# Windowed attention with sinks, then a maxout feed-forward layer: the prologue in a new order, and the stores one slot later

## The chip, the core and the metric

The kernel runs on one core of a Trainium2 chip. A core has five engines that run their own instruction streams and meet through semaphores: TensorE (PE, matrix products; its weight loads are shown as PEld), VectorE (DVE), ScalarE (ACT), GpSimd (POOL) and SyncE (SP, which here only issues transfers). Transfers (DMAs) are issued by SP, POOL and, at the end, ACT. Results of TensorE land in PSUM, of which this kernel uses eight buffers in turn; everything else lives in SBUF.

The metric is device time in microseconds (us). Before the change it is 181.4 us, the median of 4 runs from 181.05 to 181.6. A profile belongs to one of these runs.

## The reference

The attention part has 4 sequences (batch), 8 heads, 768 positions and head size 64. Each position sees the 128 positions up to and with itself, and the first 4 positions of the sequence (the sinks):

```python
scores = scale * np.matmul(q, k.transpose(0, 1, 3, 2))
is_sink = pos[None, :] < n_sink
in_window = (rel >= 0) & (rel < window)
a = softmax(np.where(is_sink | in_window, scores, -1e9))
attn = np.matmul(a, v)
x = attn.transpose(0, 2, 1, 3).reshape(3072, 512)
h = np.maximum(np.maximum(x @ w1, x @ w2), x @ w3)     # 512 -> 768
out = h @ w_out                                        # 768 -> 512
```

Inputs and the output are float32; the kernel computes with bfloat16 operands.

## The kernel before, in words

The 3072 rows are cut into 12 chunks of 256 positions, three chunks to a sequence. A chunk goes through the same steps, each a short letter in the kernel's own script (`step`, L453): K and Q (transpose k and q to `kk` and `qT`), B (open the PSUM banks of the scores with an additive mask, by matmuls against `ident`), S (scores of a pair of heads and their exponentials, tiles `st` and `e_sb`), M (mask the exponentials by a product on VectorE), Z and V (scores and values of the sinks), A (one pair of heads: probabilities times values into `o_ps`, then reciprocal and scaling on VectorE into `x_sb`), T (transpose `x_sb` to `xT`), F0 to F8 (one third of one of the three feed-forward products each, 8 matmuls into `h_ps`; weight 0 is taken by ScalarE's copy, weights 1 and 2 by VectorE's maximum), Y or W (output product `y_ps`, ScalarE's copy to `y_sb`, and the store), D (transposes of k and q by DMA), E (placing the transposed k), L (loads), X (sink keys). `Fa6` is step F6 of chunk `a`.

There is no scheduler. The whole program stands in an order written out by hand: strings of such steps (L497 to L563), mixed with casts and loads that are called by name. Every engine runs its instructions in the order in which they are issued there, and a wait at the head of an engine's stream holds up all behind it. The eight PSUM buffers are handed out in turn, so a step can also wait for the reader of an older tile.

The program has a prologue and slots. The prologue (L501 to L548) brings chunks 0, 1, 2 and 3 in. Chunk 0 comes by plain loads on SP; k and q of chunks 1 and 2 come as `runs` by transfers on POOL's queue that also cast to bfloat16 (L84), and so do the weights (L162, L170). POOL's stream is: build `ident` and the masks `msk` and `msk0` (L135 to L146), issue runs of chunk 1, v of chunk 1 and weight 0, build `sel` and `v_sink` (L178), cast the sink values `vs_raw` (L520), copy the sink keys, issue weights 1 and 2, cast v of chunk 1, issue chunk 2 and the output weight. `warm` matmuls (L124) fill PE's waits. Chunk 0's AV (`Aa0` to `Aa3`) stands before K and Q of chunk 1.

A slot i (L550 to L563) holds the feed-forward of chunk i, the AV of chunk i+1, the scores of chunk i+2, the DMA transposes of chunk i+3 and the loads of chunk i+4. Step T is 4 transposes on PE and a ScalarE copy for each half up to chunk 4 (L374), and a DMA transpose issued by SP (L375) from chunk 5 on. The store of a chunk is issued on SP at the end of its output step (L425). Slot 3 has a step order of its own (L557), with one F step more ahead of the AV and T at its end.

Of the kernel before, what the change touches and what calls it, by code (L numbers as in the profile page):

```python
# [16 lines left out]
def kernel(  # L17
# [13 lines left out]
    nc = tc.nc  # L31
    B, H, S, D = q.shape
# [3 lines left out]
    d_ff = moe_w1.shape[1]  # L36
# [14 lines left out]
    with tc.manual_schedule():  # L51
# [84 lines left out]
        for i in range(2):  # L136
            for slot, op, sign in ((1, ALU.is_ge, 1), (0, ALU.is_gt, -1)):
# [1 line left out]
                nc.gpsimd.affine_select(  # L139
                    out=m, in_=m, compare_op=op, fill=0.0, base=-sign * i,  # L140
                    pattern=[[sign, 2], [2 * sign, 64]], channel_multiplier=-2 * sign)
        nc.gpsimd.tensor_copy(msk[:, 2:4], msk[:, 0:2])
        msk0 = const.tile([128, 3, 128], BF16, name="msk0")
        nc.gpsimd.tensor_copy(msk0, msk[:, 1:4])
        for i in range(2):
            nc.gpsimd.memset(msk0[64 * i:64 * i + n_sink // 2, 0:2], 1.0)  # L146


        msb = const.tile([128, 4, 128], BF16, name="msb")
# [130 lines left out]

        sts = {}

        def score_banks(ci, pairs):

            for p in pairs:
                sts[ci, p] = [psum.tile([128, 4, 128], F32, tag="f", name="st") for _ in range(2)]
                for st in sts[ci, p] if ci < 2 else ():
                    nc.tensor.matmul(st if ci else st[:, 1:], lhsT=ident, rhs=msb if ci else msb0,  # L288
                                     start=True, stop=False, skip_group_check=True)

        def score(ci, pairs):

            b, c = divmod(ci, CPB)
            kc, kp = kk[ci % (2 * CPB)], kk[(ci - 1) % (2 * CPB)]
            half = [slice(64 * h, 64 * h + 64) for h in range(2)]
            if (ci, pairs[0]) not in sts:
                score_banks(ci, pairs)
            for p in pairs:
                st = sts[ci, p]
                qh = qT[ci % (2 * CPB)][:, :, p].rearrange("p i (n t) -> p n i t", n=2)  # L300
                parts = [(slice(1, 3), kc, 0, qh), (slice(3, 4), kc, 128, qh[:, 1])]
                if c > 0:
                    parts.insert(0, (slice(0, 1), kp, 128, qh[:, 0]))
                for sl, kx, k0, qx in parts:
                    for h, r in enumerate(half):
                        nc.tensor.matmul(st[h][:, sl], lhsT=kx[r, p, k0:k0 + 128], rhs=qx[r],  # L306
                                         start=ci >= 2, stop=True, skip_group_check=ci < 2)
            lo = 0 if c > 0 else 1
            for p in pairs:
                e = es[ci, p] = work.tile([128, 2, 4, 128], BF16, tag="e", bufs=8, name="e_sb")  # L310
                for h, st in enumerate(sts.pop((ci, p))):
                    nc.scalar.activation(e[:, h, lo:], st[:, lo:], AF.Exp, scale=scale)  # L312
# [58 lines left out]
        def xpose(ci, t):  # L371
            if t == 0:
                xTs[ci] = work.tile([128, 2, DS, 128], BF16, tag="xT", bufs=3, name="xT")
            if ci > CPB + 1:  # L374
                nc.sync.dma_start_transpose(  # L375
                    out=xTs[ci][:, t], in_=xs[ci][:, t].rearrange("p h d -> p (h d)"))
                return
            pt = psum.tile([128, DS, 128], BF16, tag="f", name="xt_ps")
            x = xs[ci][:, t].rearrange("p h d -> p (h d)")
            for ds in range(DS):  # L380
                nc.tensor.transpose(pt[:, ds], x[:, ds * 128:(ds + 1) * 128], ident)  # L381
            copy = nc.vector.tensor_copy if ci == 0 else nc.scalar.copy
            copy(xTs[ci][:, t], pt)  # L383
# [26 lines left out]
        def ffn_y(ci, ts, fbs):  # L410

            for t in ts:
                yps[ci, t] = psum.tile([128, d_model], F32, tag="f", name="y_ps")
            for part in fbs:
                for t in ts:
                    for fb in part:
                        nc.tensor.matmul(yps[ci, t], lhsT=hs[ci][:, fb, t * 128:(t + 1) * 128],  # L417
                                         rhs=wo[:, fb], start=(fb == 0), stop=(fb == FB - 1))
            for t in ts:
                if t == 0:  # L420
                    ys[ci] = work.tile([128, 2, d_model], F32, tag="y", bufs=3, name="y_sb")
                y = ys[ci]
                nc.scalar.copy(y[:, t], yps.pop((ci, t)))  # L423
                if t == 1:
                    store(y, ci, slice(0, 2))  # L425

        def ffn_y_end(ci):

# [24 lines left out]
        def step(op):  # L453
# [12 lines left out]
            elif name == "S":  # L466
                score(ci, [int(x) for x in arg])
            elif name == "B":
                score_banks(ci, [int(x) for x in arg])
            elif name == "M":  # L470
                mask(ci, [int(x) for x in arg])
            elif name == "Z":
# [11 lines left out]
                xpose(ci, int(arg))  # L484
            elif name == "F":
                ffn_h(ci, int(arg))
            elif name == "Y":
                ffn_y(ci, [int(arg)], [range(FB)])
            elif name == "W" and ci == NCH - 1:
# [4 lines left out]
        def run(text, **at):  # L494
# [3 lines left out]

        load_runs(1)  # L501
        load_v(1, nc.gpsimd)
        load_w(0, 0, 256)
        load_w(0, 256, d_ff)
        sink_v_init()
        warm(36)
        cast_qk(0, 0, 0, nc.vector)
        cast_qk(0, 1, 0, nc.vector)
# [2 lines left out]
        warm(4)  # L511
        run("Qa0 Ba01", a=0)
        cast_qk(0, 0, 1, nc.vector)
        mask_terms(msk, msb)
        cast_qk(0, 1, 1, nc.vector)
        run("Ka1 Sa01 Qa1 Ba23", a=0)
        run("Sa23", a=0)
        cast_v(0, 0, nc.vector)
        cast_v(0, 1, nc.vector)
        nc.gpsimd.tensor_copy(v_sink[:, :, 0:D], vs_raw)  # L520
        sink_k(0, nc.gpsimd.tensor_copy)
        load_w(1, 0, 256)
# [22 lines left out]
        run("Fb5 Sc23 Mc23 Fb8 Vc Ac0 Ac1 Ya0 Ya1", a=0, b=1, c=2)  # L545
        cast(4)
        run("Ac2 Ac3 Yb0 Tc0 Tc1 Kd0 Qd0 Kd1 Qd1 Yb1", b=1, c=2, d=3)
        run("Zd Sd0123 Md0123 De Lf", d=3, e=4, f=5)  # L548

        for i in range(2, NCH):  # L550
            if i + 3 < NCH:
                cast(i + 3)
            text = "Fa0 Fa1 {} Fa2 {} Zc Sc0123 Mc0123 Wa0"
            if i == 2:
                text = text.format("", "Vb Ab0 Fa3 Ab1 Xb Fa4 Ab2 Fa5 Ab3 Fa6 Dd Le Fa7 Fa8 Ya0 Ec Tb0 Tb1 Ya1")
                text = text.replace(" Wa0", "")
            elif i == CPB:  # L557
                text = text.format("Ec", "Fa3 Vb Ab0 Fa4 Ab1 Fa5 Ab2 Fa6 Ab3 Dd Le Fa7 Fa8 Tb0 Tb1")
            elif i < 0:
                text = text.format("Ec", "Vb Ab0 Fa3 Xb Ab1 Fa4 Ab2 Fa5 Ab3 Fa6 Dd Le Fa7 Tb0 Tb1 Fa8")  # L560
# [41 lines left out]
```

## Time and profile before

| Quantity | Value |
|---|---|
| Median of 4 runs | 181.4 us |
| The profiled execution | 181.6 us, with a span of 179.9 us from first to last instruction |
| PE busy | 171.3 us (95% of the span), granted clock 0.996 |
| DVE / ACT / POOL busy | 116.0 / 90.1 / 69.5 us |
| Feed-forward products, L396 | 864 matmuls, busy 103.5 us |
| Output products, L417 | 132 matmuls, busy 30.7 us |
| HBM traffic | 25.20 MB read, 6.29 MB written |

A busy share is an average over the whole run; what a change in one place is worth is read from that place. A line of the chain of waits holds a start, a duration and the work that was last to end there. A line of the timeline holds start, duration, engine, line of the code, instruction, operands and count, and in brackets how long the engine stood idle before it and for whom. Matmuls are pipelined, so the duration of a group (8 matmuls of 256 columns in 0.87 us in the chain) says more than the mean of one.

### The profile page before, as it was taken

How to read it: one execution, taken by the hardware profiler on the slowest of the kernel's cores; microseconds unless marked ns; L12 is line 12 of the kernel's file. 1: busy time of each engine (PE TensorE's matmuls, PEld its weight loads, DVE VectorE, ACT ScalarE, POOL GpSimd, SP SyncE). 2: the span in 40 equal slices, each digit the busy share in tenths (PEclk: the TensorE clock that was granted, in tenths of full speed). 3: DMA queues.
4: the chain of work that ended last, by engine and by line, in shares of the span. 5: the costliest groups of instructions: out<-in, count | busy, mean ns of one | idle time of the engine just before them, and what ended most of it. 6: DMA issues, size and time to landing. Idle time of an engine off the chain costs nothing.

```text
span 179.9 us, 4911 instructions
## 1 busy us (share of the span) xinstructions
PE 171.3 (95%) x1998; PEld 131.8 (73%) x1998; DVE 116.0 (64%) x245; ACT 90.1 (50%) x191; POOL 69.5 (39%) x121
## 2 busy tenths in 40 slices
PE   6869999999999999999999999999999999999991
PEld 6545888775697688588598688686796796796880
DVE  1786435687289189677667776786595785673551
ACT  2346852572971872951933924914736726622220
POOL 7909910657902394655023525336136200000001
PEclk9999999999999999999999999999999999999998
DMA  5999999999599998993799998999999935122404
GB/s 150 225 213 197 205 209 211 225 295 287 145 196 254 200 256 265 194 290 119 141 255 264 157 278 230 107 294 259 132 287 249 124 93 62 41 79 58 117 0 117
DMA packets 64645, 33.63 MB, mean 187 GB/s; under 512 B 26640, under 2 KB 60944, under 8 KB 64624
## 3 DMA queue, kind: packets, MB, share of 16 engines
q1 hardware_dynamic: 59520, 27.70, 66.5%
q0 software_dynamic: 4864, 5.38, 17.4%
q8 instruction: 15, 0.25, 0.6%
q10 hardware_dynamic: 240, 0.26, 0.6%
q14 instruction: 6, 0.05, 0.1%
HBM read 25.20 MB, written 6.29 MB: 175 GB/s over the span
## 4 chain that ended last, share of the span: by engine, by line
PE 84%; DMA 5%; ACT 4%; DVE 2%; POOL 2%; issue 2%; POOLq 0%; ACTq 0%
PE h_ps L396 50%; PE y_ps L417 16%; PE o_ps L358 6%; DMA runs<-in_k_dram 5%; PE st L306 3%; ACT e_sb L312 3%; DVE h_sb L402 2%; PE y_ps L436 2%; PE pt L251 1%; PE xt_ps L381 1%; PE st L288 1%; PE o_ps L345 1%; PE sk L325 1%; POOL msk L139 1%; ACT xT L383 1%
## 5 line engine op out<-in xcount | busy, mean ns | idle before, releaser
L396 PE MATMUL h_ps<-xT,w 128*128 128x256 bf16 x864 | 103.5, 273 | 0.3
L396 PEld LDWEIGHTS <-w 128*128 128x128 bf16 x864 | 81.3, 98 | 11.9 <-issue 1.4
L402 DVE TENSOR_TENSOR h_sb<-h_sb,h_ps 128x512 bf16<-128x512 bf16 x72 | 49.1, 684 | 27.1 <-PE h_ps L396 21.0
L312 ACT ACTIVATE e_sb<-st 128x512 bf16<-128x512 f32 (+1 forms) x96 | 45.2, 595 | 7.3 <-PE st L306 7.3
L400 ACT CAST h_sb<-h_ps 128x512 bf16<-128x512 f32 x36 | 22.0, 615 | 45.3 <-PE h_ps L396 45.3
L319 DVE TENSOR_TENSOR e_sb<-e_sb,msk 128x1024 bf16<-128x1024 bf16 (+1 forms) x40 | 28.7, 720 | 19.0 <-ACT e_sb L312 18.6
L203 POOL CAST qk_bf<-qk_raw 128x512 bf16<-128x512 f32 x36 | 22.7, 637 | 44.9 <-DMA qk_raw<-in_k_dram 31.9
L212 POOL CAST ve<-v_raw 64x512 bf16<-64x512 f32 x44 | 30.8, 700 | 20.9 <-DMA v_raw<-in_v_dram 18.0
L417 PE MATMUL y_ps<-wo,h_sb 128*128 128x512 bf16 x132 | 30.7, 379 | 0.3
L417 PEld LDWEIGHTS <-h_sb 128*128 128x128 bf16 x132 | 12.4, 97 | 14.0 <-issue 1.1
L366 DVE TENSOR_TENSOR x_sb<-o_ps,rc 128x256 bf16<-128x256 f32 x48 | 20.4, 425 | 1.7
L358 PE MATMUL o_ps<-ve,e_sb 128*128 128x65 bf16 x352 | 17.6, 194 | 0.6 <-DVE ve L212 0.6
L358 PEld LDWEIGHTS <-e_sb 128*128 128x128 bf16 x352 | 15.5, 97 | 2.6 <-issue 0.7
L423 ACT COPY y_sb<-y_ps 128x512 f32<-128x512 f32 x22 | 12.6, 636 | 9.6 <-PE y_ps L417 9.5
L407 POOL DMA_DIRECT2D out_dram<-y_sb x1 | 0.6, 571 | 35.1 <-ACT y_sb L447 35.1
L306 PE MATMUL st<-qT,kk 64*128 64x128 bf16 (+1 forms) x256 | 13.6, 237 | 0.2
L306 PEld LDWEIGHTS <-kk 64*128 64x128 bf16 x256 | 8.8, 94 | 4.8 <-issue 3.0
L363 DVE RECIPROCAL rc<-o_ps 128x4 f32<-128x4 f32 x48 | 8.5, 176 | 3.8 <-PE o_ps L358 3.6
L128 PE MATMUL warm<-ident 128*128 128x128 bf16 x56 | 5.2, 265 | 1.4 <-POOL ident masks.py:199 1.4
L256 ACT CAST qT<-pt 128x512 bf16<-128x512 f32 x4 | 2.1, 588 | 8.0 <-PE pt L251 8.0
L330 ACT ACTIVATE e_sink<-sk 128x256 bf16<-128x256 f32 x8 | 3.2, 395 | 5.6 <-PE sk L325 5.6
L128 PEld LDWEIGHTS <-ident 128*128 128x128 bf16 x56 | 4.6, 122 | 1.6 <-POOL ident masks.py:199 1.4
(58 smaller groups left out, 74.0 us busy)
## 6 DMA issues: line engine op xcount, KB each, us to landing
out_dram<-y_sb SPq DMA_DIRECT2D x22, 256.0 KB, 4.1
qk_raw<-in_k_dram SPq DMA_DIRECT2D x20, 256.0 KB, 4.2
qk_raw<-in_q_dram SPq DMA_DIRECT2D x20, 256.0 KB, 4.7
v_raw<-in_v_dram SPq DMA_DIRECT2D x10, 512.0 KB, 6.3
v_raw<-in_v_dram POOLq DMA_DIRECT2D x2, 512.0 KB, 10.3
w<-in_moe_w_dram POOLq DMA_DIRECT2D x2, 512.0 KB, 9.7
w<-in_moe_w_dram POOLq DMA_DIRECT2D x1, 768.0 KB, 11.7
wo<-in_moe_w_out_dram POOLq DMA_DIRECT2D x2, 384.0 KB, 12.9
```

What stands on the lines that cost most here:

```text
L203: (eng.tensor_copy if eng else nc.scalar.copy)(dst.rearrange("p i (h d) -> p h i d", d=D), src)
L212: (eng.tensor_copy if eng else nc.scalar.copy)(dst[64 * i:64 * i + 64], src[64 * n:64 * n + 64, :, i])
L306: nc.tensor.matmul(st[h][:, sl], lhsT=kx[r, p, k0:k0 + 128], rhs=qx[r], start=ci >= 2, stop=True, skip_group_check=ci < 2)
L312: nc.scalar.activation(e[:, h, lo:], st[:, lo:], AF.Exp, scale=scale)
L319: nc.vector.tensor_tensor(out=e, in0=e, in1=m, op=ALU.mult)
L358: nc.tensor.matmul(o[:, t, h], lhsT=es[ci, p][:, h, sl], rhs=ve[b % 2][:, n, 2 * p + h], start=(c == 0 and x == 0), stop=(x == len(blocks) ...
L366: nc.vector.tensor_mul(xs[ci][:, :, 2 * p:2 * p + 2], o[:, :, :, 0:D], rc.unsqueeze(3).to_broadcast([128, 2, 2, D]))
L396: nc.tensor.matmul(hp[:, f], lhsT=w_sb[wi, 2 * fp + f][:, ds], rhs=xTs[ci][:, :, ds], start=(ds == 0), stop=(ds == DS - 1))
L400: nc.scalar.copy(dst, hp)
L402: nc.vector.tensor_max(dst, dst, hp)
L417: nc.tensor.matmul(yps[ci, t], lhsT=hs[ci][:, fb, t * 128:(t + 1) * 128], rhs=wo[:, fb], start=(fb == 0), stop=(fb == FB - 1))
L423: nc.scalar.copy(y[:, t], yps.pop((ci, t)))
```

## The change

Ten edits, all of them in the order of work or in who does it:

- the copies that finish `msk` and `msk0` move from POOL to DVE, and `sink_v_init` moves to the head of POOL's issues;
- in chunk 0's preparation, the last q cast goes ahead of the second mask term;
- half of chunk 0's v casts move from DVE to POOL;
- the first two thirds of weight 1 are issued before the cast of the sink values, the last third after the v casts of chunk 1;
- 6 `warm` matmuls in place of two times 8; K of chunk 1 goes ahead of chunk 0's AV, Q of chunk 1 stands in its middle, T of chunk 0 comes after the first scores of chunk 1;
- pairs 0 and 1 of chunk 1 are masked by DVE products (M) in place of the additive matmuls (B);
- Tb comes one F step later, and `Fa7` directly after it;
- T of chunk 4 is done by DMA transposes;
- slot 3 takes the same step order as the later slots;
- stores are a step of their own (O) that lags: chunk 0's comes at the end of the prologue, and in slot i the store of chunk i-1 after the loads.

```diff
-        nc.gpsimd.tensor_copy(msk[:, 2:4], msk[:, 0:2])
+        nc.vector.tensor_copy(msk[:, 2:4], msk[:, 0:2])
...
-        nc.gpsimd.tensor_copy(msk0, msk[:, 1:4])
+        nc.vector.tensor_copy(msk0, msk[:, 1:4])
         for i in range(2):
-            nc.gpsimd.memset(msk0[64 * i:64 * i + n_sink // 2, 0:2], 1.0)
+            nc.vector.memset(msk0[64 * i:64 * i + n_sink // 2, 0:2], 1.0)
...
-        def score_banks(ci, pairs):
+        def score_banks(ci, pairs, mb=None):
...
-                for st in sts[ci, p] if ci < 2 else ():
-                    nc.tensor.matmul(st if ci else st[:, 1:], lhsT=ident, rhs=msb if ci else msb0,
+                for st in sts[ci, p] if mb is not None else ():
+                    nc.tensor.matmul(st if ci else st[:, 1:], lhsT=ident, rhs=mb,
...
-                                         start=ci >= 2, stop=True, skip_group_check=ci < 2)
+                                         start=not opened, stop=True, skip_group_check=opened)
...
-            if ci > CPB + 1:
+            if ci > CPB:
                 nc.sync.dma_start_transpose(
...
                 nc.scalar.copy(y[:, t], yps.pop((ci, t)))
-                if t == 1:
-                    store(y, ci, slice(0, 2))
...
+            elif name == "O":
+                store(ys[ci], ci, slice(0, 2))
...
+        sink_v_init()
         load_runs(1)
         load_v(1, nc.gpsimd)
         load_w(0, 0, 256)
         load_w(0, 256, d_ff)
-        sink_v_init()
...
+        cast_qk(0, 1, 1, nc.vector)
         mask_terms(msk, msb)
-        cast_qk(0, 1, 1, nc.vector)
         run("Ka1 Sa01 Qa1 Ba23", a=0)
         run("Sa23", a=0)
         cast_v(0, 0, nc.vector)
-        cast_v(0, 1, nc.vector)
-        nc.gpsimd.tensor_copy(v_sink[:, :, 0:D], vs_raw)
+        cast_v(0, 1, nc.gpsimd)
         sink_k(0, nc.gpsimd.tensor_copy)
         load_w(1, 0, 256)
-        load_w(1, 256, d_ff)
-        load_w(2)
+        load_w(1, 256, 512)
+        nc.gpsimd.tensor_copy(v_sink[:, :, 0:D], vs_raw)
         cast_v(1, 0, nc.gpsimd)
         cast_v(1, 1, nc.gpsimd)
+        load_w(1, 512, d_ff)
+        load_w(2)
         load_runs(2)
         load_v(2, nc.gpsimd)
         load_wo()
-        warm(8)
-        run("Aa0 Aa1 Aa2 Aa3", a=0)
-        warm(8)
-        run("Kb0 Qb0 Ta0 Ta1 Bb01 Sb01 Zb", a=0, b=1)
+        warm(6)
+        run("Kb0 Aa0 Aa1 Qb0 Aa2 Aa3", a=0, b=1)
+        run("Sb01 Zb", b=1)
         sink_v()
-        run("Bb23 Sb23 Fa0 Vb Ab0 Ab1 Fa3 Ab2 Ab3 Fa6 Fa1 Tb0 Tb1 Fa4", a=0, b=1)
+        run("Ta0 Ta1 Mb01 Bb23 Sb23 Fa0 Vb Ab0 Ab1 Fa3 Ab2 Ab3 Fa6 Fa1 Fa4 Tb0 Tb1 Fa7", a=0, b=1)
...
-        run("Fb0 Fb3 Fb6 Fb1 Fb4 Fa7 Fb7 Kc0 Fa2 Qc0 Fa5 Sc01 Mc01 Fa8 Zc Fb2",
+        run("Fb0 Fb3 Fb6 Fb1 Fb4 Fb7 Kc0 Fa2 Qc0 Fa5 Sc01 Mc01 Fa8 Zc Fb2",
             a=0, b=1, c=2)
...
-        run("Zd Sd0123 Md0123 De Lf", d=3, e=4, f=5)
+        run("Zd Sd0123 Md0123 De Lf Oa", a=0, d=3, e=4, f=5)
...
             if i == 2:
-                text = text.format("", "Vb Ab0 Fa3 Ab1 Xb Fa4 Ab2 Fa5 Ab3 Fa6 Dd Le Fa7 Fa8 Ya0 Ec Tb0 Tb1 Ya1")
+                text = text.format("", "Vb Ab0 Fa3 Ab1 Xb Fa4 Ab2 Fa5 Ab3 Fa6 Dd Le Oz Fa7 Fa8 Ya0 Ec Tb0 Tb1 Ya1")
                 text = text.replace(" Wa0", "")
-            elif i == CPB:
-                text = text.format("Ec", "Fa3 Vb Ab0 Fa4 Ab1 Fa5 Ab2 Fa6 Ab3 Dd Le Fa7 Fa8 Tb0 Tb1")
...
             else:
-                text = text.format("Ec", "Vb Ab0 Fa3 Xb Ab1 Fa4 Ab2 Fa5 Ab3 Tb0 Tb1 Fa6 Dd Le Fa7 Fa8")
-            run(text, a=i, b=i + 1, c=i + 2, d=i + 3, e=i + 4)
+                text = text.format("Ec", "Vb Ab0 Fa3 Xb Ab1 Fa4 Ab2 Fa5 Ab3 Tb0 Tb1 Fa6 Dd Le Oz Fa7 Fa8")
+            if i == NCH - 2:
+                text += " Oa"
+            elif i == NCH - 1:
+                text = text.replace("Oz ", "")
+            run(text, z=i - 1, a=i, b=i + 1, c=i + 2, d=i + 3, e=i + 4)
```

More of the change, by code (lines that the diff above doesn't have):

```diff
@@ L295, in score @@
             half = [slice(64 * h, 64 * h + 64) for h in range(2)]
-            if (ci, pairs[0]) not in sts:
+            opened = (ci, pairs[0]) in sts
+            if not opened:
                 score_banks(ci, pairs)
@@ L468, in step @@
             elif name == "B":
-                score_banks(ci, [int(x) for x in arg])
+                score_banks(ci, [int(x) for x in arg], msb if ci else msb0)
             elif name == "M":
@@ L554 @@
             if i == 2:
-                text = text.format("", "Vb Ab0 Fa3 Ab1 Xb Fa4 Ab2 Fa5 Ab3 Fa6 Dd Le Fa7 Fa8 Ya0 Ec Tb0 Tb1 Ya1")
+                text = text.format("", "Vb Ab0 Fa3 Ab1 Xb Fa4 Ab2 Fa5 Ab3 Fa6 Dd Le Oz Fa7 Fa8 Ya0 Ec Tb0 Tb1 Ya1")
                 text = text.replace(" Wa0", "")
-            elif i == CPB:
-                text = text.format("Ec", "Fa3 Vb Ab0 Fa4 Ab1 Fa5 Ab2 Fa6 Ab3 Dd Le Fa7 Fa8 Tb0 Tb1")
-            elif i < 0:
-                text = text.format("Ec", "Vb Ab0 Fa3 Xb Ab1 Fa4 Ab2 Fa5 Ab3 Fa6 Dd Le Fa7 Tb0 Tb1 Fa8")
-            else:
-                text = text.format("Ec", "Vb Ab0 Fa3 Xb Ab1 Fa4 Ab2 Fa5 Ab3 Tb0 Tb1 Fa6 Dd Le Fa7 Fa8")
-            run(text, a=i, b=i + 1, c=i + 2, d=i + 3, e=i + 4)
+            else:
+                text = text.format("Ec", "Vb Ab0 Fa3 Xb Ab1 Fa4 Ab2 Fa5 Ab3 Tb0 Tb1 Fa6 Dd Le Oz Fa7 Fa8")
[4 more added lines that the diff above has]
+            run(text, z=i - 1, a=i, b=i + 1, c=i + 2, d=i + 3, e=i + 4)
         for pool in (psum, work, raw, const):
```

## The prediction

> **What bounds the kernel now.** I read the chain of waits first, then the timeline of the first 26 us, then DMA share in half-microsecond stretches, the landing times of POOL's transfers, and slot 3 beside a later slot. The chain by engine and its first 20 us:
>
> ```profile
> PE 84%; DMA 5%; ACT 4%; DVE 2%; POOL 2%; issue 2%; POOLq 0%; ACTq 0%
> 4.25 0.45 POOL msk L146
> 4.70 8.52 DMA runs<-in_k_dram
> 13.22 0.04 issue
> 13.27 1.24 PE pt L251 x64
> 14.51 0.55 PE xt_ps L381 x8
> 15.06 0.86 PE st L288 x4
> 15.92 0.55 PE st L306 x12
> ...
> 18.56 0.98 PE h_ps L396 x8
> ```
>
> POOL's mask work ends at 4.70, the k runs of chunk 1 land at 13.2, and from 13.27 on PE works with hardly a gap to the end. So the time is: landing of the runs, plus PE's work after it, plus PE's later stalls. The largest stall that the change touches is in slot 3; the chain there, and then the same place in slot 6:
>
> ```profile
> 71.28 0.45 PE xt_ps L381 x8
> 71.72 0.22 PE sk L325 x4
> 71.94 0.56 PE st L306 x12
> 72.50 0.08 ACT e_sink L330
> 72.58 0.18 issue
> 72.77 0.63 ACT e_sb L312
> 73.40 0.04 issue
> 73.44 2.75 PE y_ps L417 x12
> ...
> 111.16 0.99 PE st L306 x24
> 112.16 2.75 PE y_ps L417 x12
> ```
>
> In slot 3, 2.16 us pass from the end of the F steps (71.28) to the output product (73.44); in slot 6 it is 112.16 - 110.93 = 1.23. The last three rows needed show the DMA engines around the end of chunk 0's loads (the last two columns are DMA share and GB/s):
>
> ```profile
> 8.00:8.50 0.50, 0.44 (x9) 0.32 (x6) 0.46 (x2) 0.50 (x2) 0.49 (x1) 1.00 0.85 114
> 8.50:9.00 0.50, 0.50 (x6) 0.21 (x3) 0.38 (x1) 0.50 (x2) 0.46 (x3) 1.00 0.55 93
> 9.00:9.50 0.50, 0.50 (x10) 0.27 (x8) 0.30 (x2) 0.50 (x2) 0.23 (x2) 1.00 0.90 164
> ```
>
> **The change part by part.** Call L the time at which the k runs of chunk 1 land (13.2 before).
>
> *Landing of the runs.* POOL drops two copies and two memsets, 2.89 to 4.70 = 1.81 us, and takes `sink_v_init` in, 8.53 to 9.23 = 0.70 us. The issue moves from 4.70 to about 3.6, 1.1 earlier. DVE gets the copies: the nearest rows are a 128x512 tensor-scalar of 0.28 and memsets of 0.06 to 0.11, so about 0.7 us after POOL's last select at 2.83. DVE stands idle until 3.88 there, which covers it; were they 0.4 longer, chunk 0's preparation would slip, and that has slack until L. How much of 1.1 reaches L no row shows. At least 0: the runs then share the engines earlier with chunk 0's loads, whose share is already 0.94 to 1.10 from 2.5 to 4.5. At most 1.1. The share falls to 0.85, 0.55 and 0.90 from 8.0 to 9.5, so about 0.35 us of engine time goes unused just ahead of the landing, and it stood at 0.79 to 0.85 from 4.5 to 5.5. Earlier packets can use that, so I take 0.7, nearer the upper end: L = 12.5. [...]
>
> *From L to the first F step.* Before, it is 18.49 - 13.27 = 5.22. After, PE has K 0.62, A0 and A1 0.4, Q 0.62, A2 and A3 0.4 (24 AV matmuls took 0.27 + 0.80 before, all ahead of L), and loses four mask matmuls (0.86 to 1.03). But the engines behind it set the pace. DVE has the two `kk` copies (1.29, from L+0.48), then four times reciprocal and product at the pitch 0.55 of 11.38, 11.94, 12.48, 13.03: the last x is ready at L+4.0. T waits for it: L+4.1 to 4.55. Then four B matmuls 1.0 (their banks wait for `vs` copies at L+4.4 and 4.8 and for the second and third exponentials at L+4.0 and 4.5), S 0.55, and F0 at L+6.15. That is 0.9 later relative to L. Bounds: +0.6 if x comes 0.3 earlier, +1.2 if the mask products or the ScalarE chain (Q copies 1.07, four exponentials 2.06) come between.
>
> *The two M products* are 0.69 to 0.72 each on DVE, after the xT copies, done near L+7.0; the first AV that needs them comes at L+7.2. Covered by F0 and V (0.87 + 0.23); without that cover 0.7. *Chunk 1's AV* lost 0.2 before (V waited 0.22 and one AV group took 0.59 instead of 0.48); a later start with finished v casts gives back 0.2 (0 to 0.3).
>
> *Weight 1.* Its first issue was held at 14.56 by the wait for `vs_raw` (POOL idle 4.37); now it comes after two v casts (2 x 0.64 from 9.3) and the sink key copies (0.69), about 11.4. No gain: before, the pieces landed at 20.56 and 23.1, ahead of their F steps at 22.6 and 23.74. The last third is issued after v of chunk 1 has landed (15.74, or 0.7 earlier) and been cast (2.57): about 17.7 to 18.3, needed by `Fa7` at 12.5 + 6.15 + 6.0 = 24.7. Weight 2 goes from 16.05 to about 19, chunk 2's runs from 19.36 to about 20. They queue behind what is not yet landed; before, the runs landed at 29.46 and were first used at 31.04, weight 2 at 27.75 and 31.67. Cost 0; without that queue up to 1.4 (rival B).
>
> *Tb one F step later, Fa7 after it:* the same matmuls, and still one F step between T and Fb0 over the two ScalarE copies of 1.08, so the stall of 0.24 at 24.6 stays. The swapped cast and mask term put 0.28 ahead of chunk 0's second scores, which nobody awaits before L+0.6. The 10 `warm` matmuls fewer stand in waits: 0, apart from rival C.
>
> *Stores.* Before, four stores held SP from 43.79 to 49.45 ahead of D of chunk 4 (49.55) and L of chunk 5. Without them D can start when its casts end at 46.69, about 2.8 earlier, and the loads of chunk 5 with it; POOL's 7.43 wait at 56.84 shrinks. PE's first use is S of chunk 5 at 71.9, its data placed at 67.1: gain 0. In later slots SP has T, D, L, then a store either way (L ends at 92.04, the store came at 92.14), so 0. The last stores do not move.
>
> *Slot 3.* T on PE goes (0.45), and two ScalarE copies (1.07) that held the exponentials and so the score banks. Slot 3 lasts 76.19 - 61.95 = 14.24, slot 6 of the same kind 13.14: at most 1.1 to gain. Not all of it: slot 3 starts with the masks of chunk 4 still running (62.43 to 66.17), and DVE then runs without a gap to the last maximum at 72.5. The seventh score bank waits for that maximum: output product near 72.9 instead of 73.44, a gain of 0.54. The two DMA transposes are issued when x is ready (71.1), the second 1.25 later, landing 2.5 to 3.9 after issue: 74.9 to 76.3, against F0 of slot 4 at 75.65. I take 0.5, between 0 and 0.9.
>
> **The sum.** -0.7 (L) + 0.9 - 0.2 - 0.5 = -0.5 us against the profiled execution, 181.6 (span 179.9 and 1.7 around it), which is 0.2 above the median of 181.4. Against the median: 180.9.
>
> **The rivals.**
> *A, the earlier issue buys nothing* (landing as before, 13.2): +0.9 - 0.2 - 0.5 = +0.2, 181.6. For it: latencies of 8.5, 8.3 and 9.7 for transfers behind one another look like a full queue. Against it: the idle share above.
> *B, slower: the last third of weight 1 comes late.* Place: `Fa7`, with all F steps of chunk 1 behind it on PE. Weight transfers took 6.0 to 7.8 from POOL's issue, so 18.3 gives 24.3 to 26.1 against the need at 24.7: up to 1.4, 180.9 + 1.4 = 182.3. It turns the forecast into a loss from a landing at 25.6 on. Against it: before, the same bytes in the same queue order had landed by 23.1.
>
> ```profile
> w<-in_moe_w_dram POOLq DMA_DIRECT2D x1, 256.0 KB, 6.0
> w<-in_moe_w_dram POOLq DMA_DIRECT2D x1, 512.0 KB, 7.8
> ```
>
> *C, slower: PE's clock falls.* After the 6 `warm` matmuls PE has nothing from about 10.3 to L, 2.2 us or more; before, its longest wait there was 0.93. The first 36 `warm` matmuls took 3.60 (100 ns each), later ones 8 in 0.45 (56 ns): there is a half speed. About 1.8 us if the next 3.6 us run so: 182.7. [...]
> *D, all of it lands:* L at 12.1 and slot 3 as short as slot 6 but for 0.2: -1.1 + 0.9 - 0.2 - 0.9 = -1.3, 180.1.
>
> **How the numbers follow.** Forecast 0.42 (its own range 180.4 to 181.3), A 0.20, B 0.12, C 0.10, D 0.16. A measurement of this kernel tells a difference from no change at about 0.2%, 0.36 us. Faster: 0.33 of the forecast and D, 0.49. Within: 0.09 of the forecast, half of A and 0.01 of B, 0.20. Slower: the other half of A, the rest of B, and C: 0.31. The range reaches from D to B: 180.1 to 182.3; left out are C and tails.
>
> **What would show it.** Right: runs issued near 3.6 and landed near 12.5; F0 of chunk 0 about 6.1 after the first K matmul; no T on PE near 71; slot 3 near 13.7 long. Wrong: a landing at 13 or later, a PE wait for weight 1 or 2 near 25, a granted clock below 1 after 12 us, or F0 of slot 4 waiting for xT.

## The result, and the profile after

The changed kernel is slower: a median of 182.58 us (180.81 to 185.54, 43 runs) beside 181.27 us for the kernel before (64 runs). The ratio is 1.0046, with a 95% interval of 1.003 to 1.0062; it leaves out every run more than 1.5% above the fastest of its kernel, which is 1 of the kernel before and 13 of the changed one, all 13 with a granted clock of 0.991 or less. By the means over all runs (44 with the profiled one) it is 182.75 beside 181.30. 180.9 had been forecast. The profiled execution took 182.28 us, with a span of 180.6 and a mean granted clock of 0.987. The chain of waits shows its first 20 us:

```profile
3.37 0.36 POOL sel L183 x2
3.72 8.33 DMA runs<-in_k_dram
12.05 0.04 issue
12.10 1.05 PE pt L251 x32
13.14 0.77 PE o_ps L359 x12
13.91 0.99 PE pt L251 x22
14.91 0.77 PE o_ps L359 x12
15.68 0.59 PE st L307 x12
...
18.83 0.98 PE h_ps L397 x8
```

The runs are issued 0.98 us earlier and land 1.17 us earlier (13.22 before). But the first F step is at 18.83, later than before (18.56): K's first 32 matmuls take 1.05 us, where 64 took 1.24 before. The table of stretches says why (columns: stretch and its length, busy time of PE, PEld, DVE, ACT and POOL with counts, granted clock, DMA share, GB/s):

```profile
8.00:8.50 0.50, 0.49 (x5) 0.20 (x3) 0.50 (x2) 0.50 (x3) 0.00 (x0) 1.00 0.90 135
8.50:9.00 0.50, 0.50 (x5) 0.18 (x5) 0.13 (x1) 0.50 (x3) 0.00 (x0) 1.00 0.82 151
9.00:9.50 0.50, 0.50 (x11) 0.33 (x12) 0.22 (x1) 0.50 (x2) 0.19 (x1) 1.00 1.17 199
12.00:13.00 1.00, 0.91 (x32) 0.91 (x32) 0.24 (x1) 0.00 (x0) 1.00 (x2) 0.58 1.00 261
13.00:14.00 1.00, 1.00 (x24) 0.85 (x21) 1.00 (x3) 0.00 (x0) 0.47 (x2) 0.50 1.41 196
14.00:15.00 1.00, 1.00 (x36) 0.94 (x34) 0.93 (x5) 0.47 (x1) 0.70 (x2) 0.50 1.31 204
15.00:16.00 1.00, 1.00 (x22) 0.91 (x22) 0.71 (x4) 0.60 (x2) 0.94 (x2) 0.71 1.30 224
```

The DMA share from 8 to 9.5 is higher than before (0.90, 0.82, 1.17 beside 0.85, 0.55, 0.90): the idle share was used. And the granted clock is halved from about 12.2 to 15.6 (in the kernel before it is 1.00 in these stretches), after 2.23 us in which TensorE had nothing. That is rival C. Slot 3 in the chain:

```profile
71.60 0.69 DVE h_sb L403
...
72.38 0.70 DVE h_sb L403
73.08 0.04 issue
73.12 0.38 PE st L307 x5
73.50 2.70 PE y_ps L418 x12
```

TensorE's transposes are gone from it, but the output product is at 73.50 (73.44 before): VectorE's maxima now end at 73.08. The landing of weight 1's thirds and weight 2, in the list of transfers from 11 to 18 us (bytes, us from issue to landing), and the end of the chain:

```profile
w<-in_moe_w_dram POOLq DMA_DIRECT2D x3, 256.0 KB, 8.0
w<-in_moe_w_dram POOLq DMA_DIRECT2D x1, 768.0 KB, 10.0
```

```profile
162.15 0.65 SPq L376
162.80 0.05 issue
162.85 2.85 DMA xT<-x_sb
165.70 0.14 issue
165.84 8.02 PE h_ps L397 x72
```

No F step waited for a weight. But the last chunk's F0 waited for its DMA transpose, which the kernel before does nowhere: there, 15.45 us lie between slot 9's sink exponential (149.94) and the last F0 (165.39); here 15.89.

### The profile page after: what moved, and what is told of

The parts are those of the page before. It is cut to its first block, busy times and chain, and to the rows that moved or that the text cites. A ratio compares the mean times of both kernels' runs of the same rounds, so it can differ in the third digit from the quotient of the medians.

```text
span 180.6 us, 4878 instructions
## 1 busy us (share of the span) xinstructions
PE 171.4 (95%) x1976; PEld 132.1 (73%) x1976; DVE 118.2 (65%) x249; ACT 89.5 (50%) x189; POOL 69.2 (38%) x120
## 4 chain that ended last, share of the span: by engine, by line
PE 80%; DMA 6%; DVE 5%; ACT 3%; issue 2%; POOL 1%; SPq 0%; POOLq 0%; DVEq 0%; ACTq 0%
PE h_ps L397 48%; PE y_ps L418 15%; PE o_ps L359 6%; DMA runs<-in_k_dram 5%; PE st L307 4%; DVE h_sb L403 3%; ACT e_sb L313 2%; PE pt L251 2%; DMA xT<-x_sb 2%; PE y_ps L435 2%; PE xt_ps L382 1%; PE sk L326 1%; PE o_ps L346 1%; POOL msk L139 1%; ACT xT L384 1%
## 5 line engine op out<-in xcount | busy, mean ns | idle before, releaser
L320 DVE TENSOR_TENSOR e_sb<-e_sb,msk 128x1024 bf16<-128x1024 bf16 (+1 forms) x42 | 30.6, 739 | 17.4 <-ACT e_sb L313 16.8
L359 PE MATMUL o_ps<-ve,e_sb 128*128 128x65 bf16 x352 | 18.2, 197 | 0.0
L359 PEld LDWEIGHTS <-e_sb 128*128 128x128 bf16 x352 | 16.1, 100 | 1.9
L251 PE MATMUL pt<-ident,runs 128*64 128x64 bf16 x128 | 3.5, 220 | 2.2 <-DMA runs<-in_k_dram 2.2
```

What stands on the lines that cost most here:

```text
L320: nc.vector.tensor_tensor(out=e, in0=e, in1=m, op=ALU.mult)
L359: nc.tensor.matmul(o[:, t, h], lhsT=es[ci, p][:, h, sl], rhs=ve[b % 2][:, n, 2 * p + h], start=(c == 0 and x == 0), stop=(x == len(blocks) ...
```

## The experiments

The kernels of a group ran on one chip, with the kernel before beside them, and the ratios are to its runs there; so between groups the ratio is to be compared, not the median.

### First group: one part undone, or one part alone

```diff
 e1_warm46      (changed kernel)   -warm(6)   +warm(46)
 e2_old_stores  (changed kernel)   stores again in ffn_y: + if t == 1: store(y, ci, slice(0, 2)); no steps Oa, Oz
 e3_lag_alone   (kernel before)    no store in ffn_y; + steps Oa, Oz as in the change
 e4_prologue    (changed kernel)   stores, chunk 4's T and slot 3 as before
```

> The changed kernel with 46 warm matmuls in place of 6 ahead of K of chunk 1, so that TensorE has work from 9.4 us to about 12.0, where the runs land. Theory 'gap' (the 2.2 us without work before K is what halves the clock from 12.4 to 15.5, and this is the loss): the granted clock stays at 1.0 from 12 to 16, the first 32 matmuls of K take 0.62 instead of 1.05, F0 of chunk 0 starts near 18.2 instead of 18.77, and the kernel is 0.6 to 1.3 us faster than the changed one, that is, near 181.3 beside 181.3 for the kernel before. Theory 'lag' (the loss is made by the lagged stores at the end): the clock may recover, but slots 9 and 10 wait for their transposes as they do now, and the kernel stays 0.4 to 0.8 us slower than before.

> The changed kernel with the stores back where they were before: issued with the output step, no lag. Theory 'lag': the second DMA transpose for chunk 11 lands about 0.45 us earlier (F0 of the last chunk near 165.4 instead of 165.84), POOL's casts of chunk 6 leave the masks of slot 3 alone, so slot 3 shortens by up to 0.5; in all 0.5 to 1.0 us faster than the changed kernel. Theory 'gap': no change against the changed kernel (within 0.3 us), about 0.5 to 0.8 slower than before, with the clock halved near 12 to 16 as now.

> The kernel before with the lagged stores alone. Theory 'lag': 0.3 to 0.8 us slower than before, with a wait for the transposes of chunk 11 at the last F steps. Theory 'gap': the same time as before within 0.2 us, clock as before.

> The changed kernel's prologue alone: stores, transposes of chunk 4 and the order of slot 3 as before. Theory 'gap': 0.4 to 1.0 us slower than before, clock halved for 3 us or more after the gap. Theory 'lag': the same as before within 0.2 us, since in the profile of the changed kernel slot 2 starts at 48.62 as before (48.63) in spite of the slow prologue.

| Kernel | Median us | Ratio [95%] | Clock of its runs |
|---|---|---|---|
| e1_warm46 | 182.80 | 1.0068 [1.0043, 1.0092] | 0.996 to 1.0 |
| e2_old_stores | 182.84 | 1.0035 [0.9999, 1.0071] | 0.981 to 1.0 |
| e3_lag_alone | 182.06 | 1.0047 [1.0022, 1.0071] | 0.995 to 1.0, one 0.987 |
| e4_prologue | 182.32 | 1.0021 [0.9993, 1.0049] | 0.976 to 1.0 |

With 46 warm matmuls the clock holds in every run, yet nothing is won. They ran from 10.25 to 12.92 and held K up; that explains 0.9 us at most (K at 12.92 instead of 12.0), not the whole. Two late transposes stand in its chain:

```profile
123.86 4.47 DMA xT<-x_sb
137.17 4.35 DMA xT<-x_sb
```

All four profiled executions of this group hold such places (four in e2_old_stores, one each in e3_lag_alone and e4_prologue), at another slot each time, with the old stores too. Neither "the clock" nor "the stores" covered that.

### Second group: slot 3 alone, K first alone, fewer warm matmuls

```diff
 e5_slot3            (kernel before)   -if ci > CPB + 1:  +if ci > CPB:   (T of chunk 4 by DMA)
                                       - the elif i == CPB branch         (slot 3 in the usual order)
 e6_warm28           (changed kernel)  -warm(6)   +warm(28)
 e7_prologue_warm28  (e4_prologue)     -warm(6)   +warm(28)
 e8_k_first          (kernel before)   -warm(8); run("Aa0 Aa1 Aa2 Aa3"); warm(8); run("Kb0 Qb0 Ta0 ...")
                                       +warm(6); run("Kb0 Aa0 Aa1 Qb0 Aa2 Aa3"); run("Ta0 Ta1 Bb01 Sb01 Zb")
```

> The kernel before with one part of the change: chunk 4's x is transposed by DMA, and slot 3 takes the order of the later slots. The prediction: the 0.45 us of TensorE transposes and 1.07 us of ScalarE copies go, 0.5 us faster, 181.0 beside 181.5. Rival 'DVE': slot 3 ends when VectorE's exponentials, masks and relus end, which the edit leaves alone; slot 4's F0 is where it was, 181.5 (within 0.2 us). Rival 'transposes': each further transpose in SP's queue is one more that can land late, 182.0.

> The changed kernel with 28 warm matmuls instead of 6 ahead of chunk 1's K (at 58 ns each, the time between 10.2 and 12.85 us for 46 of them, they end about 11.5 us and delay no K at 12.05). Theory 'gap': the clock is at 0.995 or above in all runs, the first K group takes 0.6 us instead of 1.05; with the prologue's 1.0 us and the stores' 0.85 us (the kernel with lagging stores alone) the sum is 181.4, the slow tail over 183.5 gone. Theory 'lag' as the only cause: the clock costs nothing in the median, 182.5 as the changed kernel.

> The changed prologue alone (stores, chunk 4's transpose and slot 3 as before), with 28 warm matmuls instead of 6. Theory 'gap': without the clock's fall the prologue is worth what its profiled execution showed, 1.0 us at the start of slot 2 and slot 3: 180.5, faster than both kernels. Theory 'transposes': an earlier start of slot 2 moves the loop against SP's queue, and late transposes of x take back what was won: 181.3 with the clock at 1.0.

> The kernel before with the reordering alone: chunk 1's K ahead of chunk 0's AV behind six warm matmuls; runs, weights, masks, casts and stores are issued as before. The runs land at 13.2 us, so TensorE waits from about 10.7 to 13.2 us. Theory 'gap': this wait lets the clock fall in most executions, to 0.98 to 0.99 over the run, K's first group 1.0 us; with F0 0.9 us later (the prediction's step), 183.0 to 183.5. Without a part of the clock: the prediction's +0.9 alone, 182.4, clock 0.995 or above.

| Kernel | Median us | Ratio [95%] | Clock of its runs |
|---|---|---|---|
| e5_slot3 | 181.11 | 0.9984 [0.9962, 1.0006] | 0.995 to 1.0 |
| e6_warm28 | 180.69 | 0.9983 [0.995, 1.0016] | 0.995 to 1.0 |
| e7_prologue_warm28 | 182.44 | 1.0041 [1.0007, 1.0076] | 0.995 to 1.0 |
| e8_k_first | 184.02 | 1.0143 [1.0097, 1.0189] | 0.981 to 1.0 |

e8_k_first shows the clock again, after 2.46 us without a matmul that ended at 12.52 (table of stretches, columns as above):

```profile
12.00:13.00 1.00, 0.48 (x18) 0.48 (x20) 0.00 (x0) 0.00 (x0) 0.21 (x1) 0.78 1.02 262
13.00:14.00 1.00, 1.00 (x33) 0.94 (x28) 0.79 (x2) 0.00 (x0) 0.96 (x6) 0.50 1.36 215
```

In e8_k_first 26.67 us pass from the landing of the runs to the sink exponential of chunk 2, against 23.45 before. A mean clock of 0.991 over 182 us accounts for at most 1.6 of these 3.2 (an equally long fall cost the changed kernel 0.85, below); for the rest, its chain goes through VectorE's products of chunk 0 (16.05 and 16.60) and eight mask matmuls, which the change's other parts take out of the way.

Twenty-two more warm matmuls bring the changed kernel from 182.5 to 180.7. By itself that would fit the clock. But e7_prologue_warm28, with a full clock in every run and slot 2 starting 0.9 us earlier than before in its profiled execution, is slower than the kernel before. A third cause had to exist.

### Third group: on one chip with the changed kernel

```diff
 e9_changed                (changed kernel, nothing edited)
 e10_warm28_2              (changed kernel)  -warm(6)  +warm(28)
 e11_warm28_slot3_before   (e10)  T of chunk 4 and slot 3 as before
 e12_warm28_stores_before  (e10)  stores as before
```

> The changed kernel itself, on one chip with the three kernels that follow. Theory 'gap' (six warm matmuls leave TensorE without work ahead of chunk 1's K, and the clock falls in a part of the executions): granted clock over the run between 0.975 and 1.0, differing from run to run, below 0.993 in at least a third of them; 182.4, 1.0 to 1.7 us over the kernel with 28 warm matmuls. Theory 'landing' (the clock costs little; what counts is how the runs and transposes land): within 0.4 us of it.

> The kernel with 28 warm matmuls again, beside the changed kernel on one chip. 'gap': clock 0.995 or above throughout, 180.9, no slower than the kernel before and 1.0 to 1.7 us below the changed kernel. 'landing': no difference from the changed kernel beyond 0.4 us.

> 28 warm matmuls, lagging stores, but chunk 4's x transposed by TensorE and slot 3 in the old order. The traces so far give 36.4 us (28 warm matmuls) beside 37.2 us (the same with stores, transpose and slot 3 as before) from chunk 3's to chunk 5's sink exponential, and 37.0 in the kernel before. If slot 3's edit is worth the 0.5 us that was predicted wherever VectorE is not stretched beside POOL's casts, this kernel is 0.5 to 0.8 us slower than the 28 warm matmuls alone: 181.5. If VectorE bounds the slot either way: the same, 180.9.

(The two marks meant there are the sink exponentials of chunks 4 and 7.)

> 28 warm matmuls, chunk 4's x by DMA and the new slot 3, but the stores where they were. If lagging stores cost what they cost alone on the kernel before (0.47%, 0.85 us), this kernel is the fastest of all: 180.1. If the stores do nothing in themselves and only the landing of transposes differs from run to run: 180.9 as with the stores lagging. If the lag is what keeps the early loop out of the transposes' way (the changed prologue with the stores as before had 182.4): 182 or above.

| Kernel | Median us | Ratio [95%] | Clock of its runs |
|---|---|---|---|
| e9_changed | 182.54 | 1.0089 [1.0052, 1.0125] | 0.977 to 1.0 |
| e10_warm28_2 | 180.85 | 0.9984 [0.9962, 1.0005] | 0.995 to 1.0 |
| e11_warm28_slot3_before | 182.34 | 1.0063 [1.0033, 1.0094] | 0.992 to 1.0 |
| e12_warm28_stores_before | 180.89 | 0.9996 [0.9958, 1.0035] | 0.991 to 1.0 |

The 1.7 us between the first two are there again. But the runs of e9_changed whose clock was 0.995 or above took 181.7 to 183.3 us; all runs of e10_warm28_2 took 180.2 to 181.7. So in this group the clock is the smaller part. Here the stores make no difference; undoing slot 3's edit costs 1.5 us, more than slot 3 was longer than a later slot (1.1).

The traces then showed what late transposes have in common. The kernel's code is itself read by DMA; the profile lists it as a queue of its own, here over the whole of the kernel before (packets, MB, share):

```profile
q8 instruction: 15, 0.25, 0.6%
```

That is 15 reads of 16 KB, about one in 11 us of the loop. In the 20 profiled executions of this case (these and those below) there are 152 pairs of DMA transposes of x. In 42 pairs such a read falls within 4 us of the issue, and in 19 of these TensorE (its matmuls or its weight loads) waits for the transpose, 0.2 to 1.0 us. In the 110 others it waits once, for 0.17 us. The landings say the same of the second transpose of a pair, where the trace has them: 9 of 27 took over 4 us with such a read, none of 51 without; of the first, 11 of 31 and 9 of 45. (The smaller reads, 8 KB each on another queue, did not matter here: 36 of the 110 have one, and none of these waits.)

The reads keep pace with TensorE. From the first of them to the last (13.38 to 160.54 us in the kernel before, 15.84 to 162.39 in the changed one) TensorE runs 3501 and 3375 matmuls and weight loads, on average 250 and 241 from one read to the next (14 intervals each). If it is TensorE's code that is read here, what counts is where the loop's instructions stand in it: their position. Every edit that adds or drops TensorE instructions moves it. It is given here as the number of TensorE instructions ahead of slot 9's first F step, less the same number in the kernel before. Counted in the built programs, it is 0 in the kernel before (4021 TensorE instructions in all), -41 in the changed one (3980), +3 with 28 warm matmuls (4024).

### Fourth group: the clock and the position apart

```diff
 e13_wide8            (changed kernel)   -warm(36)  +warm(34)
                      -warm(6)  +8 x nc.tensor.matmul(wp, lhsT=ident, rhs=msb)     (512 columns each)
 e14_before_shift16   (kernel before)    -warm(8)  +warm(16)   (the second, ahead of Kb0)
 e15_prologue_warm20  (e4_prologue)      -warm(6)  +warm(20)
 e16_changed_shift44  (changed kernel)   -warm(36)  +warm(30); warm(28, 32)        (28 of 32 columns)
```

> The changed kernel with the gap filled but no instruction more: 8 warm matmuls of 512 columns (some 1.7 us, to about 11.1 us) instead of 6 of 128, and 2 fewer in the first warm-up. TensorE's code has the changed kernel's length and positions, its clock is kept as with 28 small ones. Theory 'gap' alone: 180.85 as with 28 warm matmuls, clock 0.995 or above. Theory 'code' (a 16 KB read of TensorE's instructions that falls between a transpose of x and its landing makes it land late; 28 instead of 6 warm matmuls moved these reads off the transposes): the clock is full, but 16 KB reads stand beside the transposes near 71, 83, 96 and 161 us as in the changed kernel, TensorE waits for transposes there, 181.8 to 182.2.

> The kernel before with 8 more warm matmuls in the 0.9 us that TensorE waits for chunk 1's runs anyway (8 x 0.058 = 0.46 us): nothing else is changed, but all later TensorE code stands 16 instructions further on. That is the position (within 1 instruction) of the two kernels with the old slot 3 and 28 warm matmuls, 182.3 and 182.4. Theory 'code': 182.0 to 182.4, with a 16 KB read and a late transpose near 137 us. Without it: 181.4 as before, at most 0.2 us more where the runs land early.

> The changed prologue alone (stores, chunk 4's transpose and slot 3 as before) with 20 warm matmuls: TensorE's code in the loop stands where it does in the kernel before, to 1 instruction. With 28 it had 182.44. Theory 'code': the reads of code fall as in the kernel before, and what is left is the prologue's own gain, runs 1.05 us earlier less 0.6 us for the new order: 180.7 to 180.9. Without it: 182.4 as with 28; the clock is full in both.

> The changed kernel, gap and all, but 6 matmuls of the first warm-up are replaced by 28 of 32 columns, so that all later TensorE code stands 44 instructions further on, where it does with 28 warm matmuls ahead of K. Theory 'code' alone: 180.9. 'gap' alone: 182.5 with clocks from 0.977 to 1.0. Both: the late transposes go, the falls of the clock stay in a third to a half of the runs, 181.3.

| Kernel | Median us | Ratio [95%] | Clock of its runs |
|---|---|---|---|
| e13_wide8: gap filled, code not moved | 182.25 | 1.0054 [1.0029, 1.0079] | 0.995 to 1.0 |
| e14_before_shift16: code of before moved | 182.01 | 1.0046 [1.0021, 1.0071] | 0.995 to 1.0 |
| e15_prologue_warm20: before's position | 181.30 | 1.0005 [0.9981, 1.0028] | 0.987 to 1.0 |
| e16_changed_shift44: gap kept, code moved | 181.46 | 1.003 [1.0003, 1.0057] | 0.989 to 0.999 |

Filling the gap without moving the code brings the clock back and little time: 0.3 us by the medians, 0.6 by the ratios. (The profiled execution of e13_wide8 also lost 1.2 us ahead of chunk 2, with TensorE waiting 0.74 and 0.20 us for chunk 0's v casts, whose load landed at 12.25. How often that happens in it is not known, so it may make the clock look too cheap.) Moving the code without filling the gap brings 1.1 us. A cleaner comparison takes only runs whose clock was 0.993 or above: six of e16_changed_shift44 have a mean of 181.03, the 36 with 28 warm matmuls at the same position 181.02; six of e9_changed have 182.31, and the twelve of e13_wide8 182.50. With the clock full, it is the position that separates them.

Moving the code of the kernel before by 16 instructions, with 8 matmuls in a wait, makes it 0.7 us slower. In its profiled execution the runs landed early (12.36), so the matmuls held K up by some 0.3 us:

```profile
11.69 1.05 PE L128 MATMUL warm<-ident 128*128 128x128 bf16 x16
12.68 1.28 PE L251 MATMUL pt<-ident,runs 128*64 128x64 bf16 x64
```

That is hardly the loss: the same 8 matmuls in e17_slot3_shift16 (below), which holds K up in the same way, leave the ratio where e5_slot3 has it without them (0.9983 and 0.9984). The loss is later, and the chain shows the place. First that kernel, then the kernel before at the same slot:

```profile
133.44 1.76 PE h_ps L396 x16
135.21 0.81 SPq L375
136.02 0.04 issue
136.06 4.44 DMA xT<-x_sb
140.50 0.14 issue
140.64 1.36 PE h_ps L396 x11
```

```profile
137.10 0.61 ACT e_sb L312
137.71 0.04 issue
137.75 2.75 PE y_ps L417 x12
140.50 0.55 PE h_ps L396 x5
```

In the one, F0 waits for a transpose that takes 4.44 us; in the other it follows the output product. From chunk 10's sink exponential to chunk 11's it is 13.90 against 13.20. The same at the last slot for e9_changed and e16_changed_shift44, which differ in where the code stands and by nothing else after the first warm-up: the DMA queues of the first while the last transposes are under way (161 to 163 us), and TensorE's F step after them in its timeline,

```profile
q1 hardware_dynamic: 436, 0.11, 26.8%
q8 instruction: 1, 0.02, 3.8%
```

```profile
165.94 0.81 PE L397 MATMUL h_ps<-xT,w 128*128 128x256 bf16 x6 [0.71 <-DMA xT<-x_sb]
```

and the same of the second (160 to 162 us):

```profile
q1 hardware_dynamic: 482, 0.12, 30.5%
```

```profile
164.04 1.69 PE L398 MATMUL h_ps<-xT,w 128*128 128x256 bf16 x14
```

In the first a read of code stands beside them, and TensorE waits 0.71 us; in the second there is none, and no wait. e13_wide8, at the changed kernel's position with a full clock, waits for three transposes (here the waits by engine: us in all, times, longest):

```profile
PE h_ps L397 <- DMA xT<-x_sb: 0.8, 2, 0.5
PEld L397 <- DMA xT<-x_sb: 0.7, 1, 0.7
```

Only TensorE's instructions were moved in e14 and e16, and the 16 KB reads moved with them: the last one in the loop comes 9.78 us after chunk 11's sink exponential in e14_before_shift16 and 10.60 in the kernel before, 10.06 in e16_changed_shift44 and 12.17 in e9_changed. So these are reads of TensorE's code. All kernels by position:

| Position | Kernels (ratio to the kernel before) |
|---|---|
| -41 | e9_changed 1.0089, e13_wide8 1.0054, e2_old_stores 1.0035 |
| -27, -20 | e4_prologue 1.0021, e8_k_first 1.0143 |
| -14 | e5_slot3 0.9984 |
| 0, +1, +2 | kernel before 1, e3_lag_alone 1.0047, e15_prologue_warm20 1.0005, e17_slot3_shift16 0.9983 |
| +3 | e6, e10, e18 (28 warm matmuls) 0.9983, 0.9984, 0.9986, e12_warm28_stores_before 0.9996, e16_changed_shift44 1.003 |
| +16, +17 | e14_before_shift16 1.0046, e7_prologue_warm28 1.0041, e11_warm28_slot3_before 1.0063 |
| +39 | e1_warm46 1.0068 |

Between -14 and +3 only two kernels are slower than before by more than 0.1%: the one with lagging stores alone, and the one whose gap is left open. Outside, every kernel is, though the intervals of two (e2_old_stores, e4_prologue) reach to 1, and e8_k_first has a cause of its own. How a read of 16 KB makes a transpose late, no run here shows. The position is not all either: in 23 of the 42 pairs a read falls beside a transpose without a wait. At the slot shown above for e14_before_shift16 and the kernel before, the read falls 3.58 us after the issue in the one and 3.65 in the other, about when the transposes land; such a slot is on the edge, and one profiled execution of each is no measure of how often it tips. Nor does each trace hold its kernel's loss: the profiled execution of e7_prologue_warm28, one of its fastest (180.99), has no late transpose.

### Fifth group: what the prologue is worth

```diff
 e17_slot3_shift16  (e5_slot3)          -warm(8)  +warm(16)   (ahead of Kb0)
 e18_warm28_3       (changed kernel)    -warm(6)  +warm(28)
```

> The kernel before with the change's slot 3 and chunk 4's transpose by DMA, and 8 more warm matmuls in the wait ahead of chunk 1's runs, which puts TensorE's code in the loop within 1 instruction of the changed kernel with 28 warm matmuls. Prologue and stores are those of before. Theory 'code': no late transpose, 180.9, and what separates it from the kernel of the next run is the changed prologue alone, 0.4 us (runs 1.05 us earlier less 0.6 us). Without it: 181.6, as the same edit without the 8 matmuls (181.1) and 0.46 us for them.

> The changed kernel with 28 warm matmuls a third time, beside the last kernel on one chip: 180.75 as before (180.69, 180.85), 0.3% under the kernel before; 0.4 us faster than the last kernel if the prologue is worth what the traces say (runs 1.05 us earlier less 0.6 us), no faster if that gain is lost in the loop.

e17_slot3_shift16 had 181.46 (0.9983 [0.995, 1.0015]), e18_warm28_3 181.10 (0.9986 [0.996, 1.0011]); that edit of slot 3 is at least not slower at this position. By medians the prologue is worth 0.36 us, by the ratios nothing; a difference of that size is not settled by 12 runs each. Three times 28 warm matmuls, 36 runs, have a mean of 181.02 us; the 83 runs of the kernel before beside them 181.46. The difference is 0.44 us with a standard error of 0.13 (worked out over all runs): this version beats both kernels, by a quarter of a per cent, though no single interval leaves out 1.

### Where the time is, by marks in the traces

Marks are ScalarE's sink exponentials (`e_sink`), in us; "landing" is that of the k runs of chunk 1.

| Kernel | Landing | Landing to chunk 2 | Chunk 4 to 7 | Chunk 10 to 11 | Chunk 11 to end |
|---|---|---|---|---|---|
| kernel before | 13.22 | 23.45 | 36.99 | 13.20 | 29.96 |
| changed, first profile | 12.05 | 24.90 | 37.00 | 13.20 | 30.65 |
| e9_changed | 11.88 | 24.04 | 36.70 | 13.20 | 31.24 |
| e6_warm28 | 11.97 | 24.05 | 36.40 | 13.20 | 30.03 |
| e16_changed_shift44 | 11.85 | 24.05 | 36.50 | 13.20 | 30.07 |
| e15_prologue_warm20 | 12.60 | 24.04 | 36.99 | 13.20 | 29.97 |
| e14_before_shift16 | 12.36 | 24.10 | 36.98 | 13.90 | 29.96 |
| e3_lag_alone | 13.03 | 23.41 | 36.98 | 14.35 | 30.02 |
| e8_k_first | 12.48 | 26.67 | 37.05 | 13.21 | 29.98 |

## Why the prediction was wrong, step by step

*Landing of the runs, -0.7: right.* 1.17 in the pair of profiles, but the landing scatters by itself: 12.36 to 13.22 in the six executions with the old order on POOL, 11.33 to 12.70 in the fourteen with the new one, on average 12.68 and 12.05. That is -0.63. Rival A is out: the landing moved by two thirds of the 0.98 us by which the issue did. That the idle share let it do so fits, but no run tests it.

*From L to F0 and chunk 1's AV, +0.9 and -0.2: right in sum.* With the clock full it is 24.04 to 24.05 from landing to chunk 2's mark in the nine executions where K follows the landing, against 23.41 to 23.45 in three with the old order: +0.62, where the two steps gave +0.7. (In four others of the new order it is 24.26 to 25.43: the q runs landed late, warm matmuls or v casts held TensorE up, or it waited for chunk 2's runs.) So the prologue was forecast at 0.0 and is 0.0: an earlier K, paid for by a later F0.

*The warm matmuls, "0, apart from rival C": this step failed, twice.* First, rival C came true, and 0.10 was too low a chance. The clock was below 0.993 in 27 of the 44 runs of the result and in 5 of the 11 of e9_changed, and in none of the 36 of this kernel with 28 warm matmuls (in 2 of the 33 of its variants e7, e11 and e12). In the profiled execution it cost 0.85 us (24.90 against 24.05), about half of the rival's 1.8. The 27 runs are 1.6 us longer than the 17 others on average (183.37 and 181.78); a late landing lengthens the wait and the time alike, so not all of this need be the clock's. Over all runs of the result that makes 0.5 us (27 of 44 times 0.85) to 1.0 (times 1.6). The 0.10 was the author's estimate; no row of the kernel before shows a wait of its matmuls there of more than 0.93 us, and so none shows what a longer one does. The clock fell after 2.23 us, and after 2.46 in e8_k_first; in the profiles with waits of 1.1 to 1.8 us at this place (1.6 in e9_changed, 1.5 in e16_changed_shift44) it did not. Why it falls in some executions of the same kernel and not in others, no run here shows.

Second, and about as large, no step priced what the number of TensorE instructions does. With 10 warm matmuls, 4 mask matmuls and chunk 4's transposes gone, and others come in, the loop's code stands 41 instructions earlier at slot 9, the reads of it fall beside transposes of x, and F0 waits there. In the two profiles of the changed kernel it is 0.69 and 1.28 us longer than before from chunk 11's mark to the end, and in the second another 0.46 is lost at the first F step of slot 6. The 17 runs of the result with a full clock are 0.9 us above the 36 with 28 warm matmuls, each against the kernel before beside them; in e9_changed and e13_wide8 it is 1.1 to 1.5 on one measure or another. None of the rivals was this one.

*Slot 3, -0.5: mis-sized.* From chunk 4's mark to chunk 7's, eight executions with the old slot 3 took 36.98 to 37.21, on average 37.04. Eleven with the new one (leaving out one with two late transposes) took 36.39 to 37.08, on average 36.72: -0.3. In the first profile it was 0, and the timelines show what took it. VectorE's mask product and copy of the transposed k in the changed kernel, and POOL at that time:

```profile
65.36 1.03 DVE L320 TENSOR_TENSOR e_sb<-e_sb,msk 128x1024 bf16<-128x1024 bf16 x1
...
66.91 0.79 DVE L223 COPY kk<-kT 128x1024 bf16<-128x1024 bf16 x1
```

```profile
65.00 2.42 POOL L203 CAST qk_bf<-qk_raw 128x512 bf16<-128x512 f32 x3 [0.17 <-DMA qk_raw<-in_q_dram]
```

The same copy and POOL in e6_warm28, where POOL is done before it:

```profile
65.87 0.41 DVE L223 COPY kk<-kT 128x1024 bf16<-128x1024 bf16 x1
```

```profile
62.16 3.67 POOL L203 CAST qk_bf<-qk_raw 128x512 bf16<-128x512 f32 x4 [2.73 <-DMA qk_raw<-in_k_dram]
```

The copy takes 0.79 beside a cast and 0.41 alone, a mask product 1.03 instead of 0.80 (the same product in the kernel before and in e6_warm28). (In the kernel before it was POOL that gave way: the copy took 0.41 and the two casts beside it 0.71 each instead of 0.61.) The slot ends with VectorE, so this goes into it, and when POOL casts depends on when loads land. In the profiles of e5_slot3 and e12_warm28_stores_before TensorE waited 0.25 and 0.41 us for chunk 4's transpose, which DMA now makes, beside a read of code: another way to lose it.

*Stores, 0: right as far as it goes.* At position +3 (e10 and e12) and at -41 (changed kernel and e2_old_stores) the lag makes no difference. Alone on the kernel before it costs 0.47%; in its profile a transpose landed 4.90 us after its issue, beside a read of code (1.15 more from chunk 10 to 11). Why there only is open.

*Weight 1, 0:* right; rival B did not come. *Rival D* was nearly reached, at another position: e6_warm28's profile has a span of 178.6.

The sum with measured terms, for the runs of the result: -0.6 + 0.6 - 0.3 + 0.5 to 1.0 (clock) + 0.9 (position) = +1.1 to +1.6, against +1.45 by the means, +1.3 by the medians and +0.84 by the ratio. The reasoning about the prologue stood; the sign came from two things outside it.

## What to carry to other kernels

In this kernel 16 TensorE instructions more moved the 16 KB reads of its code: the last one in the loop came 9.78 us after chunk 11's mark instead of 10.60, and the kernel was 0.46% slower. Where a transfer has little slack, test an edit that adds or drops such instructions at two or three positions (a few matmuls more in a wait) before judging it. When work is taken out ahead of a wait of TensorE, look at the granted clock after that wait, over several runs: a wait of 2.23 us was enough here. Fill it only as far as the wait goes (28 matmuls gave 0.9983 to 0.9986 with a clock of 0.995 or above in all 36 runs, 46 held K up by 0.9 us and gave 1.0068), and mind that the filler moves the code too.

## What was not expected of the hardware

- 16 KB reads of TensorE's code (15, 0.25 MB in all) and DMA transposes: 19 of 42 pairs of transposes with such a read within 4 us of the issue kept TensorE waiting, and 1 of 110 without.
- Eight matmuls of 0.06 us in a wait of TensorE, nothing else, made the kernel before 0.46% slower [0.21%, 0.71%].
- The granted clock halved after 2.23 and 2.46 us without a matmul, for 3.4 us each time; in the profiles with waits of 1.1 to 1.8 us there it did not.
- The landing of one 8 us transfer scatters by 0.9 to 1.4 us between executions with the same order of POOL's issues.
